# An attention-and-MLP kernel on one core: the halves of the weights are made by ScalarE and VectorE, GpSimd's casts go to other engines, and the planner that writes the order prices TensorE by the kind of product

## The chip, the cores and the metric

The kernel runs on one core of a Trainium2 chip. A core has five engines that run side by side, each with a queue of its own that is worked strictly in order: TensorE (PE in the profile, with its weight loads as PEld), VectorE (DVE), ScalarE (ACT), GpSimd (POOL) and SyncE (SP), which here only issues DMAs. The metric is the device time of one execution in microseconds (us), as the median of several runs.

## The reference

```python
def _attn_ref(q, k, v, M_prev, z_prev, beta):          # B, H, S, D = 4, 8, 576, 64
    scores = np.matmul(q, k.transpose(0, 1, 3, 2)) / np.sqrt(D)
    scores = np.where(np.triu(np.ones((S, S), bool), k=1), -1e9, scores)
    a = np.exp(scores - scores.max(-1, keepdims=True))
    a /= a.sum(-1, keepdims=True) + 1e-09
    local = np.matmul(a, v)
    q_p = np.where(q > 0, q, np.exp(q) - 1.0) + 1.0
    mem_out = (np.einsum('bhsd,bhde->bhse', q_p, M_prev)
               / (np.einsum('bhsd,bhd->bhs', q_p, z_prev)[..., None] + 1e-06))
    g = 1.0 / (1.0 + np.exp(-beta))[None, :, None, None]
    return g * mem_out + (1 - g) * local

def _moe_ref(x, w_in, w_out):                          # x: 2304 x 512, w_in: 512 x 2048, w_out: 2048 x 512
    h = x @ w_in
    return (h * np.cos(h)) @ w_out
```

The attention's output, laid out as 2304 tokens of 512 values, is the input x of the second part. Both weights come as 64-bit floats.

## The kernel before

**Stages and tiles.** The 2304 tokens are worked as nine chunks of 256: the first 64 rows of every head of all four batches (`small_pair`), then two chunks for each batch (`heads`, `scores`, `parts`, `local`, `memory`). While one job's attention is made, the second part (`moe_chunk`) runs for the chunks of the job before. A chunk is cut into eight **units** of 256 hidden columns, so that there are 72 units, counted from 1 here. Unit n is: a first product on TensorE into a PSUM bank `u` (`unit1`, L852); then a chain in `hidden`: ScalarE rounds (L873), VectorE subtracts (L875), ScalarE takes the sine (L877), VectorE multiplies by `u` (L879, the unit's **last multiply**), a cast makes the high half `gh` (by `copy`, L358 on ScalarE or L360 on the others) and a subtraction the low half `gl` (`sub`, L368); then a second product into `acc` (`unit2`, L894). There are two banks `u`, and a unit's last multiply still reads its bank: **the first product of unit n+2 cannot begin before the last multiply of unit n has ended.**

**Halves.** Eight chunks (64 units) use products of `fp32r` operands, each number cut in a high and a low half, three products for one. The first chunk (units 1 to 8, made while weights arrive) uses whole fp32 products. Each of 32 weight blocks is loaded as 64-bit words (`load_w`: DMA into `ws`; GpSimd's clamp L468; ScalarE L471; VectorE's shift L473; VectorE's join into `weight_val`, L478, from two SBUF tensors). `split_w` later cuts it into `weight_high` (L496 on ScalarE or L498 elsewhere) and `weight_low` (L503).

**Sine and exponential** need different tables on ScalarE, so a change between them costs an `ACT_TABLE_LOAD`.

**Order.** `Plan` collects all operations with the engines that may do each and a cost for each, and `order` lays them out by a simulated schedule; what comes out is the order in which every engine's queue is written, and which engine does each operation. `prm` has the numbers that steer it; `phi_on`, `gh_on` and `gl_on` are lists of the engines that may do a cast or a subtraction. A queue never reorders afterwards: a late operand holds all that stands behind it.

Of the kernel before, what the change touches and what calls it, by code (L numbers as in the profile page):

```python
# [37 lines left out]
class Op:  # L38
    __slots__ = ("on", "eng", "move", "tail", "share", "fn", "prio", "deps", "table", "idx", "start", "left", "outs", "at", "done", "cost", "port")
# [244 lines left out]
def kernel(  # L288
# [233 lines left out]
    def scores(prio, r, pair, qs, kcols, W, mk, nbs, sms, c):  # L522
# [5 lines left out]
        for k0 in range(0, W, n):  # L528
# [8 lines left out]
            P.op({"PE": 200 + 4 * mm(n)}, prod, prio, r=[pair], w=svs)  # L537
# [42 lines left out]
    def values(prio, stv, m, h, v2):  # L580
# [9 lines left out]
        def total(e):  # L590
            with nc.allow_low_precision("only the power of two next to the sum is used"):
# [4 lines left out]
             prio, r=[sums], w=[sv], after=[o_const], tail=106.0)  # L596
# [35 lines left out]
    def memory(prio, xbs, h0, nh, terms, reads, bank):  # L632
# [37 lines left out]
    def local(prio, rr, xbs, h, got, sm, r0, vals, mems):  # L670
# [140 lines left out]
    def emit_xT(prio, xbs, split):  # L811
# [7 lines left out]
        for b, xb in enumerate(xbs):  # L819
# [19 lines left out]
    def unit1(prio, i, bufs, views, split):  # L839

        u = P.buf("u")
        j, c0 = divmod(2 * i, 4)
        for f in range(2):
            cs = (c0 + f) * 128

            def prod(e, f=f, cs=cs):
# [39 lines left out]
    def unit2(prio, i, bufs, views, acc, split):  # L886
        for b in range(2):
# [211 lines left out]
```

## Time and profile before

| | |
|---|---|
| median of 3 runs | 611.62 us (608.96 to 611.73) |
| the profiled execution, own time | 612.86 us |
| its span, first to last instruction | 611.1 us |
| TensorE busy | 576.5 us, 94%, 4441 records |
| VectorE busy | 414.1 us, 68% |
| ScalarE busy | 367.9 us, 60% |
| GpSimd busy | 312.5 us, 51% |

Busy shares are averages over stages with different limits, so they name no bound by themselves. A VectorE or GpSimd row's duration includes time in which the instruction has been started and is held up.

### The profile page before, as it was taken

The numbers are of one execution on the slowest core, as the hardware profiler recorded it, in microseconds if no ns is written. First come the engines' busy times: TensorE is split into PE (matmuls) and PEld (weight loads), VectorE is DVE, ScalarE is ACT, GpSimd is POOL, SyncE is SP. The second block draws the span as 40 slices with busy tenths as digits, with TensorE's granted clock in tenths as the row PEclk, the third lists the DMA queues.
The fourth block names the chain that finished last, engine by engine and source line by source line (L and its number), as shares of the span: only waits on it lengthen the run. The fifth ranks groups of instructions, "written<-read, shape, count | busy, mean of one in ns | idle before, by whom it ended". The sixth has DMA issues, their size and how long they took to land.

```text
span 611.1 us, 12464 instructions
## 1 busy us (share of the span) xinstructions
PE 576.5 (94%) x4441; PEld 463.2 (76%) x4441; DVE 414.1 (68%) x1235; ACT 367.9 (60%) x798; POOL 312.5 (51%) x372
## 2 busy tenths in 40 slices
PE   6872699999999999999999999999999999999997
PEld 4661466567887877867987888888878889899996
DVE  3889989899788789887487856566878452322221
ACT  4857558688986788775576565576766532322321
POOL 3498477787665554653456263446453522332432
PEclk9876599999999999999999999999999999999999
DMA  8687885547663568548062843251833140000000
GB/s 277 212 207 217 252 243 157 106 86 172 142 136 69 145 143 150 118 98 178 19 149 64 158 84 84 39 136 49 146 58 85 39 64 1 35 1 1 35 1 35
DMA packets 121870, 67.07 MB, mean 110 GB/s; under 512 B 104656, under 2 KB 110288, under 8 KB 121808
## 3 DMA queue, kind: packets, MB, share of 16 engines
q1 hardware_dynamic: 121808, 66.28, 46.1%
q8 instruction: 35, 0.57, 0.4%
q14 instruction: 27, 0.22, 0.1%
HBM read 36.37 MB, written 4.72 MB: 67 GB/s over the span
## 4 chain that ended last, share of the span: by engine, by line
PE 83%; ACT 4%; DMA 4%; DVE 3%; issue 2%; POOL 2%; SPq 0%; POOLq 0%; ACTq 0%; DVEq 0%
PE u L852 33%; PE acc L894 32%; PE S L534 8%; PE pv L680 5%; PE mm L646 3%; DMA t<-p 2%; DMA ws<-in_w_in 2%; PE mm L824 1%; ACT s L549 1%; DVE p L562 1%; POOL wt L468 1%; DVE weight_val L478 1%; DVE wt L473 1%; SPq L371 0%; POOL weight_low L503 0%
## 5 line engine op out<-in xcount | busy, mean ns | idle before, releaser
L562 DVE SCALAR_TENSOR_TENSOR p<-s,p 128x64 f16<-128x64 f32 (+4 forms) x256 | 115.7, 489 | 18.9 <-POOL p L360 17.2
L852 PE MATMUL u<-xh,weight_high 128*128 128x256 f32 x416 | 120.5, 290 | 0.3 <-DVE w L879 0.3
L852 PE MATMUL u<-xl,weight_high 128*128 128x256 f32 x416 | 115.9, 279 | 0.0
L852 PE MATMUL u<-xh,weight_low 128*128 128x256 f32 x416 | 115.9, 279 | 0.0
L360 POOL TENSOR_SCALAR p<-s 128x320 f16<-128x320 f32 (+3 forms) x107 | 62.2, 586 | 97.0 <-ACT s L549 58.8
L360 POOL TENSOR_SCALAR gh<-w 128x512 fp32r<-128x512 f32 x58 | 38.2, 659 | 139.7 <-DVE w L879 94.9
L873 ACT ACTIVATE w<-u 128x512 int32<-128x512 f32 x72 | 42.7, 593 | 96.7 <-PE u L852 77.7
L894 PE MATMUL acc<-weight_high,gh 128*128 128x512 f32 x240 | 98.0, 409 | 0.0
L875 DVE SCALAR_TENSOR_TENSOR w<-w,u 128x512 f32<-128x512 int32 x72 | 48.9, 679 | 70.8 <-ACT w L873 70.8
L894 PE MATMUL acc<-weight_low,gh 128*128 128x512 f32 x240 | 94.5, 394 | 0.0
L894 PE MATMUL acc<-weight_high,gl 128*128 128x512 f32 x240 | 94.2, 393 | 0.0
L549 ACT ACTIVATE s<-s,nb 128x448 f32<-128x448 f32 (+3 forms) x128 | 77.8, 611 | 26.5 <-DVE nb L541 25.9
L852 PEld LDWEIGHTS u<-xh,weight_high 128*128 128x128 f32 x416 | 78.3, 188 | 10.7 <-issue 7.2
L368 POOL TENSOR_TENSOR gl<-w,gh 128x512 fp32r<-128x512 f32 x64 | 83.2, 1301 | 5.4 <-ACT gh L358 1.2
L852 PEld LDWEIGHTS u<-xl,weight_high 128*128 128x128 f32 x416 | 78.4, 188 | 1.0
L852 PEld LDWEIGHTS u<-xh,weight_low 128*128 128x128 f32 x416 | 78.5, 189 | 0.0
L534 PE MATMUL S<-stq 64*128 64x288 f32 (+3 forms) x320 | 66.3, 479 | 5.7 <-DVE nb L541 5.6
L541 DVE CUSTOM_DVE_ANT_0 s<-S,mask 128x320 f32<-128x320 f32 (+3 forms) x128 | 57.7, 474 | 18.6 <-PE S L534 18.1
L877 ACT ACTIVATE w<-w 128x512 f32<-128x512 f32 x72 | 45.1, 631 | 30.6 <-DVE w L875 30.3
L894 PEld LDWEIGHTS acc<-weight_high,gh 128*128 128x128 f32 x240 | 45.1, 188 | 16.4 <-issue 7.2
L879 DVE TENSOR_TENSOR w<-w,u 128x512 f32<-128x512 f32 x64 | 43.5, 680 | 19.9 <-ACT w L877 19.8
L680 PEld LDWEIGHTS <-t 128*128 128x128 f16 x1216 | 39.1, 98 | 18.1 <-issue 10.7
(116 smaller groups left out, 1093.4 us busy)
## 6 DMA issues: line engine op xcount, KB each, us to landing
ws<-in_w_in SPq DMA_DIRECT2D x16, 512.0 KB, 5.0
ws<-in_w_out SPq DMA_DIRECT2D x16, 512.0 KB, 3.9
stq<-in_qkp SPq DMA_DIRECT2D x12, 544.0 KB, 4.3
stv<-in_vk SPq DMA_DIRECT2D x16, 320.0 KB, 3.4
out<-w SPq DMA_DIRECT2D x16, 256.0 KB, 2.1
t<-p SPq DMA_TRANSPOSE x128, 3.2
mz<-in_mzp SPq DMA_DIRECT2D x20, 66.0 KB, 2.8
stq<-in_qkp SPq DMA_DIRECT2D x4, 288.0 KB, 3.4
```

Source lines behind the costliest of these rows:

```text
L360: eng[e].tensor_scalar(out=out, in0=in_, scalar1=scale, scalar2=1.0, op0=ALU.mult, op1=ALU.mult)
L368: lambda e: eng[e].tensor_tensor(out=out, in0=in0, in1=in1, op=ALU.subtract), prio, port=kw.pop('port', True), **kw)
L534: nc.tensor.matmul(out=sv.ap[:, 0:n], lhsT=pair.ap[p, qs], rhs=pair.ap[p, kcols + k0:kcols + k0 + n], start=True, stop=True)
L541: nc.vector.tensor_tensor_reduce(out=st.ap[:, k0:k0 + n], in0=sv.ap[:, 0:n], in1=mk[:, k0:k0 + n], scale=-1.0 / math.sqrt(D), scalar=above ...
L549: ex.append(P.op({"ACT": act(W, False, 2)}, lambda e, st=st, nb=nb, sm=sm: nc.scalar.activation(out=st.ap[:, 0:W], in_=st.ap[:, 0:W], func ...
L562: Pp({"DVE": dve(n)}, lambda e, c=c, n=n, to=to: nc.vector.scalar_tensor_tensor(out=pt.ap[:, to:to + n], in0=sa[:, c:c + n], scalar=PSCALE ...
L680: nc.tensor.matmul(out=pv.ap[:, 64 * i:64 * i + 64], lhsT=got[r].ap[:, block, :], rhs=vals.ap[:, part, h % 2, 64 * j:64 * j + 64], start=( ...
L852: nc.tensor.matmul(out=u.ap[:, f, :], lhsT=a[:, cs:cs + 128], rhs=x, start=(n == 0), stop=(n == len(terms) - 1))
L875: P.op({"DVE": dve(512)}, lambda e: nc.vector.scalar_tensor_tensor(out=wv, in0=wi, scalar=0.25, in1=u.ap, op0=ALU.subtract, op1=ALU.subtra ...
L877: P.op({"ACT": act(512, False)}, lambda e: nc.scalar.activation(out=wv, in_=wv, func=ACTF.Sin, scale=-TWO_PI_BELOW), ep, w=[w], table="sin")
L879: P.op({"DVE": dve(512)}, lambda e: nc.vector.tensor_tensor(out=wv if split else views[0], in0=wv, in1=u.ap, op=ALU.mult), ep, r=[u], w=[w ...
L894: nc.tensor.matmul(out=acc[b].ap, lhsT=a, rhs=w, start=(i == 0 and f == 0 and n == 0), stop=(2 * i + f == NF - 1 and n == len(terms) - 1))
```

## The change

It does four things. `some` and the new lists `hi_on`, `lo_on` and `clamp_on` fix who cuts the weights: ScalarE makes every high half, VectorE every low half, GpSimd keeps the clamps. The casts of `parts` and `hidden` (`phi_on`, `gh_on`) may no longer go to GpSimd. In the planner, a change of TensorE between kinds of product (`SWITCH`, whole fp32, halves, scores, small fp16) now has a price whenever the kind changes, and several costs are set anew. And the steering numbers in `prm` are others. The computation is the same.

```diff
+SWITCH = {"h": 0.0, "v": 15.0}
...
-                back = e == "PE" and tail == 80.0 and o.tail != 80.0
+                back = e == "PE" and o.kind != kind
...
             if e == "PE":
-                if o.tail != 80.0:
-                    cost += tail
-                tail = o.tail
+                cost += SWITCH.get(o.kind, 95.0) if o.kind != kind else 0.0
+                kind = o.kind
...
+    def some(on, name):
+        return {e: on[e] for e in on if e in prm[name]}
...
-        P.op({"Pool": pool(512), "DVE": dve(512)}, lambda e: eng[e].tensor_scalar(
+        Pp(some({"Pool": pool(512), "DVE": dve(512)}, "clamp_on"), lambda e: eng[e].tensor_scalar(
...
-        o = P.op({"ACT": act(512, False), "DVE": dve(512, True), "Pool": pool(512)}, high, prio,
-                 after=[w_ready[key], *left_by.get(ph, list)()])
-        w_ready[key] = Pp({"DVE": dve(512), "Pool": 1240}, low, prio, after=[o, *left_by.get(pl, list)()])
+        o = Pp(some({"ACT": act(512, False), "DVE": dve(512, True), "Pool": pool(512)}, "hi_on"), high, prio,
+               after=[w_ready[key], *left_by.get(ph, list)()])
+        w_ready[key] = Pp(some({"DVE": dve(512), "Pool": 1240}, "lo_on"), low, prio, after=[o, *left_by.get(pl, list)()])
...
-    "xt": 12.861,
...
+    "xt": 24.853,
...
-    "phi_on": ('ACT', 'Pool', 'DVE'),
-    "gh_on": ('ACT', 'Pool', 'DVE'),
+    "phi_on": ('ACT', 'DVE'),
+    "gh_on": ('ACT', 'DVE'),
     "gl_on": ('DVE', 'Pool'),
+    "hi_on": ('ACT',),
+    "lo_on": ('DVE',),
+    "clamp_on": ('Pool',),
```

The built programs show who does what now. GpSimd's queue falls from 372 rows to 176: its casts by `copy` from 175 to 19, its high and low halves of weights (12 and 32) to none. ScalarE's casts by `copy` rise from 41 to 176 and its high halves from 20 to 32; its table loads fall from 56 to 50 and its scalings of `x` (L666) from 96 to 60. VectorE gets 32 low halves, 21 casts, 18 scalings of two heads at once (L662) and 5 instructions of L623. TensorE has the same 4057 products in both, in 293 runs of one kind before and 297 now. DMAs are the same in number. Lines of the changed kernel are 3 to 9 higher than those of before (L885 is L879 of before, L883 is L877, L509 is L503, L474 is L468).

GpSimd's queue from its fourth clamp on, before (`wt` is the block being made from `ws`, `p` an attention tile, `stv` and `v` a tile of values):

```order
L468 TENSOR_SCALAR wt_139<-ws_137 128x512
L498 TENSOR_SCALAR weight_high<-weight_val 128x512
L503 TENSOR_TENSOR weight_low<-weight_val,weight_high 128x512
L498 TENSOR_SCALAR weight_high<-weight_val 128x512
L360 TENSOR_SCALAR p_90<-s_78 128x320
L468 TENSOR_SCALAR wt_138<-ws_134 128x512
L503 TENSOR_TENSOR weight_low<-weight_val,weight_high 128x512
L360 TENSOR_SCALAR p_92<-s_74 128x192
L468 TENSOR_SCALAR wt_139<-ws_135 128x512
```

and the same place of the change:

```order
L474 TENSOR_SCALAR wt_139<-ws_137 128x512
L474 TENSOR_SCALAR wt_138<-ws_134 128x512
L474 TENSOR_SCALAR wt_139<-ws_135 128x512
L474 TENSOR_SCALAR wt_138<-ws_136 128x512
L474 TENSOR_SCALAR wt_139<-ws_137 128x512
L474 TENSOR_SCALAR wt_138<-ws_134 128x512
L474 TENSOR_SCALAR wt_139<-ws_135 128x512
L610 TENSOR_SCALAR stv_67<-stv_67,vs_108 128x384
L363 TENSOR_SCALAR v_72<-stv_67 128x2x192
```

The halves and casts that stood between the clamps have left the queue, so a clamp follows the clamp before.

ScalarE's queue around the first sine, before (`w_102` and `w_103` are the tiles of units 1 and 2; the rounding of unit 1, L873, stands 30 rows ahead of its sine, and 18 of the 32 weight blocks' L471 stand ahead of it):

```order
L358 ACTIVATE p_92<-s_74 128x192
L549 ACTIVATE s_75,sm_121<-s_75,nb_117 128x192
L592 ACTIVATE v_72,va_113<-stv_67 128x385
L877 ACT_TABLE_LOAD
L877 ACTIVATE w_102<-w_102 128x512
L471 ACTIVATE wt_138<-wt_138 128x512
L877 ACTIVATE w_103<-w_103 128x512
```

and in the change, where 12 of the L471 (now L477) stand ahead of it:

```order
L361 ACTIVATE p_93<-s_75 128x192
L879 ACTIVATE w_102<-u_128 128x512
L627 ACTIVATE e_69<-stq_66 128x256
L477 ACTIVATE wt_139<-wt_139 128x512
L632 ACTIVATE e_69<-e_69 128x256
L883 ACT_TABLE_LOAD
L883 ACTIVATE w_102<-w_102 128x512
L477 ACTIVATE wt_138<-wt_138 128x512
L502 CAST weight_high<-weight_val 128x512
```

The sine of unit 1 has moved up to five rows behind its rounding.

VectorE's queue around the last multiply of unit 8 (the sixth row), before (`xl` is the low half of the next chunk's input, the ISA rows are the maxima of scores):

```order
L879 TENSOR_TENSOR t_88<-w_102,u_128 128x512
L541 ISA s_87,nb_114<-S_130,mask,nb_114 128x288
L541 ISA nb_114 128x1
L473 TENSOR_SCALAR wt_139<-wt_139 128x512
L368 TENSOR_TENSOR xl_101<-mm_133,xh_100 128x4x128
L879 TENSOR_TENSOR t_89<-w_103,u_129 128x512
L478 SCALAR_TENSOR_TENSOR weight_val<-ws_137,wt_139 128x512
L541 ISA s_86,nb_115<-S_131,mask,nb_115 128x288
```

and from that multiply on in the change:

```order
L885 TENSOR_TENSOR t_89<-w_103,u_129 128x512
L509 TENSOR_TENSOR weight_low<-weight_val,weight_high 128x512 x2
L371 TENSOR_TENSOR xl_101<-mm_133,xh_100 128x4x128
L547 ISA s_87,nb_114<-S_130,mask,nb_114 128x288
L547 ISA nb_114 128x1
L547 ISA s_86,nb_115<-S_131,mask,nb_115 128x288
L547 ISA nb_115 128x1
L509 TENSOR_TENSOR weight_low<-weight_val,weight_high 128x512 x2
```

Low halves stand there now, where none was. Ahead of the last multiply of unit 13, VectorE's two lists differ by 26 low halves, 6 scalings of two heads (12 for 6) and one cast more, and by one each of L875, L628, L601 and L575 less. Ahead of the first product of unit 15 TensorE's lists differ by 25 small products of `local` (204 for 229), and ahead of that of unit 19 by nothing but their order.

## Rows read from the trace of the kernel before

**Rows 1.** The page, part 1: busy time, share of the span and instructions of each engine.

```profile
PE 576.5 (94%) x4441; PEld 463.2 (76%) x4441; DVE 414.1 (68%) x1235; ACT 367.9 (60%) x798; POOL 312.5 (51%) x372
```

**Rows 2.** Busy time of each engine in four stretches; the columns are the stretch, its length, busy us (and instructions) of TensorE, its weight loads, VectorE, ScalarE and GpSimd, the granted clock, the share of the DMA engines' time, and GB/s.

```profile
37.00:69.30 32.30, 15.05 (x72) 10.80 (x72) 28.63 (x55) 20.86 (x45) 26.51 (x27) 0.66 0.77 218
69.30:169.30 100.00, 98.34 (x609) 68.72 (x610) 88.89 (x237) 74.43 (x157) 68.92 (x74) 0.97 0.65 160
169.30:287.60 118.30, 116.69 (x1033) 90.77 (x1032) 99.54 (x338) 87.63 (x194) 62.92 (x77) 1.00 0.60 129
287.60:500.00 212.40, 212.40 (x1806) 177.41 (x1804) 143.53 (x459) 132.29 (x280) 102.08 (x124) 1.00 0.43 86
```

**Rows 3.** TensorE in order of time, around the first product of unit 3: start, length, line, tiles, count and, in brackets, the idle time ahead and what ended it.

```profile
63.39 0.58 PE L680 MATMUL pv<-v,t 128*128 128x64 f16 x8 [3.35 <-DVE x L687]
...
69.30 6.59 PE L852 MATMUL u<-s,weight_val 128*128 128x256 f32 x16 [3.05 <-DVE t L879]
```

**Rows 4.** ScalarE in order of time, 42 to 70 us: the rounding of unit 1, the twelfth L471, and the first sine with its table load.

```profile
42.67 0.60 ACT L873 ACTIVATE w<-u 128x512 int32<-128x512 f32 x1 [0.80 <-PE u L852]
...
50.14 0.63 ACT L471 ACTIVATE wt<-wt 128x512 f32<-128x512 f32 x1 [0.22 <-POOL wt L468]
...
66.60 1.28 ACT L877 ACT_TABLE_LOAD   x1
67.89 0.63 ACT L877 ACTIVATE w<-w 128x512 f32<-128x512 f32 x1
```

**Rows 5.** VectorE in order of time, 43 to 71 us: a shift and a join held up, the last multiply of unit 1, and a shift, a division and a join that are not held up.

```profile
45.31 1.49 DVE L473 TENSOR_SCALAR wt<-wt 128x512 int32<-128x512 int32 x1
...
47.51 1.76 DVE L478 SCALAR_TENSOR_TENSOR weight_val<-ws,wt 128x512 int32<-128x512 int32 x1
...
68.56 0.69 DVE L879 TENSOR_TENSOR t<-w,u 128x512 f32<-128x512 f32 x1 [1.03 <-ACT w L877]
...
69.29 0.42 DVE L473 TENSOR_SCALAR wt<-wt 128x512 int32<-128x512 int32 x1
69.63 0.22 DVE L562 SCALAR_TENSOR_TENSOR p<-s,p 128x64 f16<-128x64 f32 x1
69.76 0.68 DVE L478 SCALAR_TENSOR_TENSOR weight_val<-ws,wt 128x512 int32<-128x512 int32 x1
```

**Rows 6.** VectorE, the last multiply of unit 13, and TensorE, the first product of unit 15, each in order of time.

```profile
168.62 0.68 DVE L879 TENSOR_TENSOR w<-w,u 128x512 f32<-128x512 f32 x1
174.70 0.28 PE L852 MATMUL u<-xh,weight_high 128*128 128x256 f32 x1
```

**Rows 7.** Busy time in three more stretches, columns as in rows 2.

```profile
30.00:169.30 139.30, 116.96 (x700) 81.92 (x700) 124.52 (x301) 100.31 (x214) 101.72 (x108) 0.89 0.68 175
134.90:151.00 16.10, 14.70 (x135) 11.47 (x133) 14.73 (x43) 14.32 (x32) 11.99 (x12) 1.00 0.76 162
0.00:287.60 287.60, 256.74 (x1921) 189.24 (x1922) 241.76 (x730) 208.00 (x473) 176.06 (x212) 0.93 0.66 164
```

**Rows 8.** Groups by form, VectorE from 0 to 150.9 us and GpSimd from 0 to 169.3 us; count | busy us, mean ns of one | idle before, and what ended it.

```profile
L478 DVE SCALAR_TENSOR_TENSOR weight_val<-ws,wt 128x512 int32<-128x512 int32 x32 | 32.4, 1014 | 0.0
L473 DVE TENSOR_SCALAR wt<-wt 128x512 int32<-128x512 int32 x32 | 19.2, 600 | 2.2 <-ACT wt L471 2.2
L562 DVE SCALAR_TENSOR_TENSOR p<-s,p 128x64 f16<-128x64 f32 x23 | 11.3, 493 | 0.7 <-ACT p L358 0.7
L875 DVE SCALAR_TENSOR_TENSOR w<-w,u 128x512 f32<-128x512 int32 x11 | 7.4, 676 | 1.6 <-ACT w L873 1.6
L575 DVE TENSOR_SCALAR sm<-sm,vs 128x2 f32<-128x2 f32 x10 | 5.7, 578 | 0.0
L503 POOL TENSOR_TENSOR weight_low<-weight_val,weight_high 128x512 fp32r<-128x512 f32 x28 | 38.9, 1391 | 2.6 <-PE acc L894 1.4 <-DMA t<-p 0.5 <-ACT weight_high L496 0.5
L468 POOL TENSOR_SCALAR wt<-ws 128x512 f32<-128x512 f32 x32 | 24.2, 757 | 28.7 <-DMA ws<-in_w_in 11.1 <-DVE weight_val L478 9.5 <-DMA ws<-in_w_out 5.2
L498 POOL TENSOR_SCALAR weight_high<-weight_val 128x512 fp32r<-128x512 f32 x10 | 7.0, 700 | 4.6 <-DMA ws<-in_w_in 1.6 <-DVE weight_val L478 1.6 <-PE mm L595 0.7
L360 POOL TENSOR_SCALAR p<-s 128x320 f16<-128x320 f32 x5 | 2.9, 588 | 1.9 <-ACT s L549 1.8
```

**Rows 9.** Groups by form over the whole span, of operations that the change adds or takes away; columns as in rows 8.

```profile
L368 DVE TENSOR_TENSOR xl<-mm,xh 128x512 fp32r<-128x512 f32 x16 | 11.0, 689 | 13.8 <-ACT xh L835 13.8
L662 DVE TENSOR_TENSOR x<-mm,r 128x128 f32<-128x128 f32 x20 | 4.8, 282 | 0.1
L680 PE MATMUL pv<-v,t 128*128 128x64 f16 x1216 | 43.4, 194 | 9.2 <-DMA t<-p 5.9 <-DVE x L687 3.3
L358 ACT ACTIVATE p<-s 128x320 f16<-128x320 f32 x7 | 3.2, 462 | 3.2 <-DMA t<-p 3.2
L496 ACT CAST weight_high<-weight_val 128x512 fp32r<-128x512 f32 x18 | 11.0, 612 | 4.7 <-DVE weight_val L478 4.2 <-POOL wide_both L503 0.5
L666 ACT ACTIVATE x<-mm,r 128x64 f32<-128x64 f32 x88 | 20.1, 310 | 2.5 <-DVE r L656 1.8 <-PE pv L680 0.5
L877 ACT ACT_TABLE_LOAD x28 | 35.9, 1283 | 0.5
```

**Rows 10.** ScalarE in order of time, the sine of unit 25, and TensorE, the first product of unit 27.

```profile
286.62 0.63 ACT L877 ACTIVATE w<-w 128x512 f32<-128x512 f32 x1
289.27 0.37 PE L852 MATMUL u<-xh,weight_high 128*128 128x256 f32 x1
```

More of the change, by code (lines that the diff above doesn't have):

```diff
@@ L38 @@
 class Op:
-    __slots__ = ("on", "eng", "move", "tail", "share", "fn", "prio", "deps", "table", "idx", "start", "left", "outs", "at", "done", "cost", "port")
+    __slots__ = ("on", "eng", "move", "kind", "share", "fn", "prio", "deps", "table", "idx", "start", "left", "outs", "at", "done", "cost", "port")
 ENGINES = ("PE", "DVE", "ACT", "Pool", "SP")
@@ L96, in buf, with op @@
         return made[-1]
-    def op(self, on, fn, prio, r=(), w=(), a=(), after=(), move=None, table=None, tail=0.0, share=1.0, port=False):
+    def op(self, on, fn, prio, r=(), w=(), a=(), after=(), move=None, table=None, kind="f", share=1.0, port=False):
         o = Op()
-        o.on, o.move, o.fn, o.prio, o.table, o.tail, o.share, o.port = on, move, fn, prio, table, tail, share, port
+        o.on, o.move, o.fn, o.prio, o.table, o.kind, o.share, o.port = on, move, fn, prio, table, kind, share, port
         deps = set(after)
@@ L194, in forward @@
         skipped = dict.fromkeys(engines, 0.0)
-        clock, queues, tail = Clock(), 0.0, 0.0
+        clock, queues, kind = Clock(), 0.0, None
         port = 0.0
@@ L535, in prod @@
                                      rhs=pair.ap[p, kcols + k0:kcols + k0 + n], start=True, stop=True)
-            P.op({"PE": 200 + 4 * mm(n)}, prod, prio, r=[pair], w=svs)
+            P.op({"PE": 194 + 4 * mm(n)}, prod, prio, kind="s", r=[pair], w=svs)
             for i, (sv, st, nb) in enumerate(zip(svs, sts, nbs)):
@@ L595, in values @@
         P.op({"PE": 3}, lambda e: nc.tensor.matmul(out=sv.ap[:, 0:1], lhsT=ones.to_broadcast([128, 128]), rhs=sums.ap, start=True, stop=True),
-             prio, r=[sums], w=[sv], after=[o_const], tail=106.0)
+             prio, r=[sums], w=[sv], after=[o_const], kind="v")
         o = P.op({"DVE": 100}, lambda e: nc.vector.tensor_scalar(
@@ L646, in prod @@
                     nc.tensor.matmul(out=mb.ap[p, c], lhsT=a, rhs=b, start=True, stop=True)
-        P.op({"PE": 10 + 4 * n / 2.4 * nb if whole else 610 + fm * mm(256)}, prod, prio, r=reads, w=[mb],
+        P.op({"PE": 1.38 * n * nb if whole else 610 + fm * mm(256)}, prod, prio, r=reads, w=[mb],
              share=1.0 if whole else (240 + fm * mm(256)) / (610 + fm * mm(256)))
@@ L682, in prod @@
                                      stop=(n == len(terms) - 1))
-        P.op({"PE": 3 + 29 * sum(3 * r + 2 for r in rr)}, prod, prio, r=[vals, *(got[r] for r in rr)], w=[pv], tail=80.0)
+        P.op({"PE": 3 + 29 * sum(3 * r + 2 for r in rr)}, prod, prio, r=[vals, *(got[r] for r in rr)], w=[pv], kind="h")
         for i, r in enumerate(rr):
@@ L824, in tr @@
                     nc.tensor.transpose(mb.ap[:, k * 128:(k + 1) * 128], xb.ap[:, k * 128:(k + 1) * 128], ident)
-            P.op({"PE": 440}, tr, prio, r=[xb], w=[mb], after=[o_const])
+            P.op({"PE": 358}, tr, prio, r=[xb], w=[mb], after=[o_const])
             mv = mb.ap.rearrange("p (k t) -> p k t", k=KD)
@@ L853, in prod @@
                                      stop=(n == len(terms) - 1))
-            o = P.op({"PE": 1380 if split else 1728}, prod, prio, r=bufs, w=[u],
+            o = P.op({"PE": 1368 if split else 1718}, prod, prio, kind="r" if split else "f", r=bufs, w=[u],
                      after=[w_ready["i", j, k] for k in range(KD)])
@@ L1009 @@
 prm = {
-    "v": -0.17,
-    "step": 1.238,
-    "pv": 2,
-    "xt": 12.861,
-    "ew": 0,
-    "u2": 13.132,
+    "v": -0.833,
+    "step": 1.165,
+    "pv": 1.318,
+    "xt": 24.853,
+    "ew": 0.517,
+    "u2": 13.369,
     "w0": -4.023,
-    "wdt": 18.984,
-    "small": 3.264,
-    "t0": 80,
+    "wdt": 23.471,
+    "small": 4.859,
+    "t0": 55.948,
     "dtu": 5.006,
     "dth": 2.0,
-    "lead": 0.917,
-    "mem": 3.906,
+    "lead": 0,
+    "mem": 4.581,
     "switch": 1300.0,
-    "patience": 60,
-    "hold": 24.207,
-    "bdve": 1140.609,
+    "patience": 19.426,
+    "hold": 32.243,
+    "bdve": 1238.886,
     "bact": 440.469,
     "ws": 0,
-    "s0": -60,
-    "rounds": 6,
+    "s0": -69.122,
+    "rounds": 11,
     "nwt": 2,
-    "glue": 0,
-    "portw": 3.0,
+    "glue": -0.185,
+    "portw": 13.204,
     "group": 4,
     "clamps": 'p',
-    "lazy": 4000,
+    "lazy": 4288.524,
     "wide": 23,
```

4 lines of the change are left out of this document (2 added, 2 removed).

## The prediction

> **What bounds the kernel now.** I read the busy times first. TensorE is busy 576.5 us of the 611.1 us span [rows 1], so the time is TensorE's work plus the waits inside it. The stretches then say where the waits are [rows 2]: from 37 to 69.3 us TensorE works 15.1 of 32.3 us, at a granted clock of 0.66 (a mixture of its two levels, 1.2 and 2.4 GHz), from 69.3 to 169.3 us it works 98.3 of 100, and from 287.6 to 500 us all 212.4. From 75 us on it is a queue that nearly always has work; whatever moves the end must move that queue as a whole.
>
> What starts the full stretch is seen in order of time. Unit 3's first product starts at 69.30 us, after 3.05 us idle, released by a last multiply [rows 3]. This is unit 1's. Its sine ran at 67.89, behind a table load at 66.60, though its rounding was done at 43.3 [rows 4], and the multiply at 68.56 [rows 5]: for 23 us it stood in ScalarE's list behind other work, weight blocks (L471) among it. The twelfth L471 ran at 50.14 [rows 4]; 18 stand ahead of the sine.
>
> TensorE being full after 75 us doesn't mean that VectorE has time to spare. A unit's first product waits for a last multiply two units back, and when the list is laid out tightly the slack is small. Unit 13's last multiply ended at 169.30 and unit 15's first product, which waits for it, started at 174.70 [rows 6]: 5.4 us. So VectorE is nearly as full as TensorE there: from 30 to 169.3 us it is busy 124.5 of 139.3 us, idle 10.6%; in its tightest part, 134.9 to 151 us, 14.73 of 16.10, idle 8.5% [rows 7].
>
> Part of that busy time is being held up. A join (L478) takes 1.76 us and a shift (L473) 1.49 where GpSimd works, and 0.68 and 0.42 at 69 us, when nothing is in the way [rows 5]. To 150.9 us the means are 1014 ns for 32 joins and 600 for 32 shifts, 493 for 23 small divisions (L562; 220 free [rows 5]), 578 for 10 tiny ones (L575; I take 220 as for L562) [rows 8]: 32 x 0.334 + 32 x 0.18 + 23 x 0.273 + 10 x 0.358 = 10.7 + 5.8 + 6.3 + 3.6 = 26.4 us.
>
> **The change part by part.** *The early start.* In the new list the sine of unit 1 stands 5 rows behind its rounding and behind 12 L471. If the rounding ends near 43.3 and the twelfth L471 near 50.8 as now [rows 4], the multiply is done near 49 to 51 and unit 3 may start some 18 to 20 us before 69.3. By itself that is a lead of up to 20 us; only what cannot hold the lead takes it away again.
>
> *VectorE has to keep up with it.* Up to the last multiply of unit 13 its list gains 26 low halves; the nearest row of that shape is the low half `xl`, 689 ns [rows 9]: 17.9 us. Six more scalings of two heads at 0.282 [rows 9] are 1.7; one cast is bounded by nothing and the 0.69 us of the same shape, I take 0.3. One each of four small kinds fewer (0.68 for L875 [rows 8], the others bounded by 0.22 and 0.6) take 2.1 off. Sum +17.8 us.
>
> *What GpSimd no longer does.* To 169.3 us it loses 32 low halves at 1391 ns (44.5), 12 high halves at 700 (8.4) [rows 8] and about ten casts at 0.6 (6): 59 us. Its clamps stay, 32 at 757 ns. How much of VectorE's held-up time goes with them I bound from two sides. Held-up time of 26.4 us against 101.7 us of GpSimd's work [rows 7] is 0.26 us for each; 59 us less gives 15. If instead a low half holds up an instruction of VectorE by 1.07 us, as at 45 and 47 us (1.49 less 0.42, 1.76 less 0.68 [rows 5]), 26 of them give 28. I take the middle, 22, since the four groups aren't all that is held up but low halves don't always meet something.
>
> *The sum.* VectorE from 30 us to the multiply of unit 13: 124.5 + 17.8 - 22 = 120.3 us of work. With 10% idle, as now, that lasts 133.7 us and ends at 163.7 instead of 169.3. The multiply no longer has 5.4 us of slack, since TensorE with 20 us lead is waiting: unit 15 starts at 163.8, 10.9 us earlier than 174.70. TensorE's list ahead of it is 25 small products of `local` shorter (25 x 43.4/1216 = 0.9 [rows 9]), which come later: a lead of 10.0 us that is worth anything. So TensorE gets 20 us of lead near 50 us and loses half of it, in waits for last multiplies between about 110 and 165 us.
>
> Behind unit 15, six low halves remain for VectorE, which is 4 us, and its shares fall (99.5 of 118.3 us, then 143.5 of 212.4 [rows 2]). TensorE's work after it is the same set of products. I count its 297 runs of one kind against 293 as nothing: from 287.6 to 500 us it turns from kind to kind and is still busy all the time [rows 2]. The DMAs are the same in number and their share falls from 0.77 to 0.43 [rows 2].
>
> *ScalarE.* To the sine of unit 25 (286.62 us [rows 10]) it gains some 58 casts, at 0.46 (320 wide) to 0.61 us (512 wide) [rows 9]: 32; 12 high halves at 0.612: 7.3; it loses 24 scalings at 0.31, 7.4, and six table loads at 1.283, 7.7. Together +24 on 208.0 us of 287.6 [rows 7]. The cover is the idle time of 79.6 us. With the lead of 10 us, it would have to do 232 in 277 us, idle 45; I count it at nothing, and take it up as a rival.
>
> *Sum of it all.* Span 611.1 - 10.0 = 601.1 us. The profiled execution's own time is 612.86, 1.8 over its span and 1.2 over the median of 611.62: so own 602.9 and a median near **601.5 us**. With relief of 15 and 10% idle, VectorE's work is 127.3 us, the multiply ends at 171.4 and the gain is 174.7 - 171.5 - 0.9 = 2.3 (609). With 28 and 8% idle it is 114.3, ends at 154.2, gain 19.5 (592).
>
> **The rivals.** *A: VectorE keeps up.* Low halves go into the idle 10%, or the relief is the full 28: the whole 20 us stays, span 591, median about 591.5. For it: a lead of 20 us moves VectorE's work earlier too, where it has some slack (28.6 of 32.3 us busy from 37 to 69.3 [rows 2]; little). Against it: the 8.5% of the tightest part [rows 7], which looks like a floor.
>
> *B: the low halves wait as the joins do.* A join reads two SBUF tensors and takes 1014 ns on average; L875 of the same shape has one operand in PSUM and takes 676 over the same stretch [rows 8]. `xl`, my row for the low half, also reads PSUM; the low half on VectorE reads `weight_val` and `weight_high`, both in SBUF. At 1014 instead of 689, 26 cost 8.5 us more, which makes 128.8 us of work, ends at 173.1, and gives unit 15 at 173.3: 1.4 less 0.9, so 0.5 us, and a median of 611. Against it: what the joins wait for is mostly the low halves that GpSimd no longer makes; only clamps are left to collide with. The Trainium skill, "SBUF — State Buffer", section "Who interferes with whom", says that VectorE and GpSimd share one pair of SBUF ports under an exclusive lock; by that rule two engines working on SBUF tensors take turns and a half moved to VectorE would not be free of waits while clamps run. The rows of joins at 1.76 beside and 0.68 us free agree with it, and by it alone the sum would lie between mine and this rival's.
>
> *C: slower, ScalarE.* The casts of `gh` may go to ScalarE or VectorE alone, and GpSimd no longer catches what is late. The place is the stretch up to unit 25's sine; unit 27's first product starts at 289.27, 2.0 us after that sine's end [rows 10]. With 232 us of work it is late as soon as its idle time there is above 57 us of the present 79.6 (289 - 232). ScalarE now idles 28% (79.6 of 287.6); at 22.5% it would end at 232 / 0.775 = 299, ten late: span 621, median 621. For it: a queue in strict order idles when an operand is late, and each `gh` cast waits for a multiply of a VectorE that I hold to be the bound. Against: its idle time is mostly not on the chain now, since from 169.3 us on TensorE is kept full while ScalarE idles a quarter (87.6 of 118.3 busy [rows 2]).
>
> *D: the early start does not come.* The first 12 L471 wait for clamps, and these for `ws` from DMA; if blocks land late, unit 3 stays near 60 to 65 us. That costs nothing as long as it takes less than the half of the lead that I count as lost anyway; it belongs to the lower half of my own range.
>
> **How the numbers follow.** My forecast (VectorE paces units 11 to 24, gain 2 to 19 us) 0.57, A 0.15, B 0.16, C 0.12. Within 0.5%, about what a measurement of this kernel can tell from no change, is 608.6 to 614.7. Faster is A and my own case but for 0.02 at its upper end: 0.70. Slower is C but for 0.02 of mild delays, and 0.02 of B, where some of C meets it: 0.12. The rest is the same: 0.18. The range has to leave out no more than 2 in 10: from 590, under A, to 612, over B; C is left out, as is a tail below.
>
> **What would show it.** The early start: unit 3's first product near 50 us, and the full clock well before 75 us. The relief: joins at 750 to 800 ns instead of 1014, shifts near 450 instead of 600, GpSimd busy 160 to 190 us instead of 312.5. The price: low halves near 0.69 us each (1.0 is B). The pacing: TensorE's longest waits between 110 and 165 us, released by a last multiply (L885), and unit 15 at about 164. If unit 15 starts there at 155, it is A. After it TensorE should need the same 436 us to the end (611.1 - 174.7); if it needs more, with waits behind sines or `gh` casts between 170 and 290 us, C is right. My forecast would be wrong most easily in the relief, which is a difference of two bounds far apart, and in taking TensorE's work as unchanged when its order is not.

## The result and the profile after

The changed kernel takes 588.58 us (median of 4 runs, 587.38 to 590.20) against 611.67 (608.96 to 613.57): a ratio of 0.9627, 95% interval 0.9584 to 0.9671. That is 23 us faster, where 10 were forecast with a range of 590 to 612. The profiled execution took 588.59 us, with a span of 586.9.

The page, part 1 and the clock row of part 2, answering to [rows 1]:

```profile
PE 568.5 (97%) x4441; PEld 457.7 (78%) x4441; DVE 402.8 (69%) x1311; ACT 415.6 (71%) x898; POOL 171.5 (29%) x172
...
PEclk9989999999999999999999999999999999999999
```

Windows of the changed kernel, columns as in [rows 2], the same four stretches, and four up to the last multiply of unit 13, which now ends at 146.6 us, to set beside [rows 7]:

```profile
37.00:69.30 32.30, 29.32 (x151) 20.65 (x150) 28.19 (x72) 24.19 (x51) 13.83 (x17) 1.00 0.94 270
69.30:169.30 100.00, 99.06 (x743) 70.87 (x742) 94.57 (x287) 88.90 (x186) 35.32 (x34) 1.00 0.61 145
169.30:287.60 118.30, 116.12 (x1034) 93.01 (x1033) 97.13 (x352) 97.49 (x220) 35.61 (x30) 1.00 0.64 130
287.60:500.00 212.40, 210.08 (x1759) 176.35 (x1758) 133.38 (x443) 144.57 (x302) 55.76 (x46) 1.00 0.38 76
0.00:30.00 30.00, 23.83 (x207) 16.82 (x208) 22.64 (x113) 24.14 (x81) 7.99 (x25) 0.97 0.88 289
30.00:146.60 116.60, 112.67 (x704) 79.29 (x702) 106.24 (x312) 98.56 (x208) 43.81 (x49) 0.98 0.77 198
0.00:146.60 146.60, 136.51 (x909) 96.11 (x909) 128.88 (x424) 122.70 (x287) 51.81 (x74) 0.98 0.79 216
110.00:146.60 36.60, 36.60 (x315) 29.23 (x311) 34.81 (x107) 33.30 (x65) 13.50 (x11) 1.00 0.62 137
```

The kernel before had up to the same multiply, and in its first 30 us:

```profile
0.00:30.00 30.00, 23.09 (x191) 16.55 (x191) 17.70 (x95) 20.06 (x69) 11.42 (x28) 0.89 0.75 249
0.00:169.30 169.30, 140.05 (x890) 98.47 (x891) 142.22 (x395) 120.37 (x281) 113.14 (x135) 0.89 0.69 188
```

From 37 to 69.3 us TensorE works 29.3 us instead of 15.1, at a granted clock of 1.00 instead of 0.66, so at 2.4 GHz throughout. Most of the time came from this stretch. From 110 us to the multiply TensorE is busy all the time, and VectorE 34.81 of 36.60 us; the next wait of TensorE for a last multiply comes behind 169.3 us (0.8 us, once). From 169.3 to 500 us TensorE is busy a little less than before, so something was given back there.

ScalarE in order of time, from the rounding of unit 1 over the twelfth L477 to the sine (before: [rows 4]):

```profile
39.87 0.58 ACT L879 ACTIVATE w<-u 128x512 int32<-128x512 f32 x1
...
40.66 0.62 ACT L477 ACTIVATE wt<-wt 128x512 f32<-128x512 f32 x1
...
41.60 1.28 ACT L883 ACT_TABLE_LOAD   x1
42.89 0.63 ACT L883 ACTIVATE w<-w 128x512 f32<-128x512 f32 x1
```

TensorE in order of time, the first products of units 1, 3 and 4 (the second answers to [rows 3]):

```profile
31.61 5.44 PE L858 MATMUL u<-s,weight_val 128*128 128x256 f32 x16
...
44.91 3.62 PE L858 MATMUL u<-s,weight_val 128*128 128x256 f32 x16
...
51.79 1.46 PE L858 MATMUL u<-s,weight_val 128*128 128x256 f32 x6
```

The sine starts 3 us after its rounding instead of 25, and the twelfth L477 runs at 40.66 us instead of 50.14 [rows 4]. Unit 1 starts 5.3 us earlier (31.61 against 36.92), unit 3 24.4 us earlier, and its product takes 3.62 us instead of 6.59, so unit 4 starts 27.4 us earlier (51.8 against 79.2).

VectorE by form, 0 to 150.9 us (before: [rows 8]):

```profile
L484 DVE SCALAR_TENSOR_TENSOR weight_val<-ws,wt 128x512 int32<-128x512 int32 x32 | 22.5, 704 | 0.0
L509 DVE TENSOR_TENSOR weight_low<-weight_val,weight_high 128x512 fp32r<-128x512 f32 x23 | 17.5, 780 | 0.0
L479 DVE TENSOR_SCALAR wt<-wt 128x512 int32<-128x512 int32 x32 | 14.5, 456 | 7.2 <-ACT wt L477 7.0
L881 DVE SCALAR_TENSOR_TENSOR w<-w,u 128x512 f32<-128x512 int32 x14 | 9.5, 678 | 0.3 <-ACT w L879 0.2
L568 DVE SCALAR_TENSOR_TENSOR p<-s,p 128x64 f16<-128x64 f32 x29 | 7.2, 248 | 2.0 <-ACT p L361 1.9
```

Joins fell from 1014 to 704 ns, nearly the 0.68 us of a free one, shifts from 600 to 456, and small divisions from 493 to 248. L881, which reads one operand from PSUM, is where it was (678 against 676). The low halves take 780 ns in the mean.

VectorE, a low half and the last multiply of unit 13, and TensorE, the first product of unit 15, in order of time (before: [rows 6]):

```profile
145.35 0.69 DVE L509 TENSOR_TENSOR weight_low<-weight_val,weight_high 128x512 fp32r<-128x512 f32 x1
145.96 0.68 DVE L885 TENSOR_TENSOR w<-w,u 128x512 f32<-128x512 f32 x1
```
```profile
145.98 1.02 PE L540 MATMUL S<-stq 64*128 64x448 f32 x4
146.94 0.39 PE L858 MATMUL u<-xh,weight_high 128*128 128x256 f32 x1
```

Unit 15 starts 27.8 us earlier, 0.3 us behind the multiply, and without a wait: TensorE is at work on scores until then. From there to the end of the span it takes 440.0 us instead of 436.4.

### The profile page after: what moved, and what is told of

It is laid out like the page before. It is cut to its first block, busy times and chain, and to the rows that moved or that the text cites. A ratio compares the mean times of both kernels' runs of the same rounds, so it can differ in the third digit from the quotient of the medians.

```text
span 586.9 us, 12402 instructions
## 1 busy us (share of the span) xinstructions
PE 568.5 (97%) x4441; PEld 457.7 (78%) x4441; DVE 402.8 (69%) x1311; ACT 415.6 (71%) x898; POOL 171.5 (29%) x172
## 4 chain that ended last, share of the span: by engine, by line
PE 66%; ACT 13%; DMA 9%; DVE 6%; issue 3%; POOL 1%; ACTq 0%; POOLq 0%; SPq 0%; DVEq 0%
PE u L858 27%; PE acc L900 26%; DMA t<-p 6%; PE S L540 5%; PE pv L686 4%; ACT s L555 3%; ACT p L361 2%; DVE p L568 2%; PE mm L652 2%; DMA ws<-in_w_out 1%; DVE s L547 1%; ACT wt L477 1%; DMA stv<-in_vk 1%; ACT L883 1%; DMA ws<-in_w_in 1%
## 5 line engine op out<-in xcount | busy, mean ns | idle before, releaser
L568 DVE SCALAR_TENSOR_TENSOR p<-s,p 128x64 f16<-128x64 f32 (+4 forms) x256 | 93.0, 403 | 11.1 <-ACT p L361 10.1
L881 DVE SCALAR_TENSOR_TENSOR w<-w,u 128x512 f32<-128x512 int32 x72 | 49.2, 683 | 73.3 <-ACT w L879 73.3
L555 ACT ACTIVATE s<-s,nb 128x192 f32<-128x192 f32 (+3 forms) x128 | 77.8, 609 | 5.3 <-DVE nb L547 5.0
L879 ACT ACTIVATE w<-u 128x512 int32<-128x512 f32 x72 | 42.5, 590 | 52.2 <-PE u L858 44.5
L361 ACT ACTIVATE p<-s 128x320 f16<-128x320 f32 (+3 forms) x114 | 55.2, 504 | 15.7 <-DMA t<-p 15.6
L540 PE MATMUL S<-stq 64*128 64x288 f32 (+3 forms) x320 | 64.8, 473 | 0.6 <-DVE nb L547 0.6
L885 DVE TENSOR_TENSOR w<-w,u 128x512 f32<-128x512 f32 x64 | 43.7, 684 | 25.6 <-ACT w L883 25.1
L883 ACT ACTIVATE w<-w 128x512 f32<-128x512 f32 x72 | 45.2, 631 | 21.8 <-DVE w L881 21.5
L361 ACT ACTIVATE gh<-w 128x512 fp32r<-128x512 f32 x57 | 35.7, 628 | 26.7 <-DVE w L885 18.9
L900 PEld LDWEIGHTS acc<-weight_low,gh 128*128 128x128 f32 x240 | 45.1, 188 | 9.7
```

The source lines that it names most:

```text
L361: nc.scalar.activation(out=out, in_=in_, func=ACTF.Copy, scale=scale)
L540: nc.tensor.matmul(out=sv.ap[:, 0:n], lhsT=pair.ap[p, qs], rhs=pair.ap[p, kcols + k0:kcols + k0 + n], start=True, stop=True)
L555: ex.append(P.op({"ACT": act(W, False, 2)}, lambda e, st=st, nb=nb, sm=sm: nc.scalar.activation(out=st.ap[:, 0:W], in_=st.ap[:, 0:W], func ...
L568: Pp({"DVE": dve(n)}, lambda e, c=c, n=n, to=to: nc.vector.scalar_tensor_tensor(out=pt.ap[:, to:to + n], in0=sa[:, c:c + n], scalar=PSCALE ...
L879: P.op({"ACT": act(512)}, lambda e: nc.scalar.activation(out=wi, in_=u.ap, func=ACTF.Copy, bias=0.25), ep, r=[u], w=[w])
L881: P.op({"DVE": dve(512)}, lambda e: nc.vector.scalar_tensor_tensor(out=wv, in0=wi, scalar=0.25, in1=u.ap, op0=ALU.subtract, op1=ALU.subtra ...
```

## The experiments

Two questions were put: does the early start last by itself, or only because VectorE got time back; and how much work could VectorE and ScalarE still take. Six kernels change the lists, the numbers or the pricing and let the planner lay the order out anew; the six others keep an order and change only who issues an instruction, or how often. Their ratios are to the kernel before in the same series (612 us).

The form of the edits in an unchanged order (here for the low halves; `high` and `"ACT"` answer to it elsewhere):

```diff
     with tc.manual_schedule():
+        for o in seq:
+            if o.fn.__name__ == "low":
+                o.eng = "Pool"
         for o in seq if not DRY else []:
             o.fn(o.eng)
```

**New lists alone, laid out anew** (`hi_on`, `lo_on`, `clamp_on`, `phi_on`, `gh_on` of the change, with `some` that reads them, put into the kernel before):

```diff
...
-    "phi_on": ('ACT', 'Pool', 'DVE'),
-    "gh_on": ('ACT', 'Pool', 'DVE'),
+    "phi_on": ('ACT', 'DVE'),
+    "gh_on": ('ACT', 'DVE'),
+    "hi_on": ('ACT',),
+    "lo_on": ('DVE',),
+    "clamp_on": ('Pool',),
```

> The kernel before with the new lists of engines alone (ScalarE makes the high halves, VectorE the low ones, GpSimd only clamps, no casts on GpSimd); steering numbers and the pricing of TensorE's changes of kind are those of before, and the planner lays the list out anew. Theory 1 (relief: what GpSimd no longer does frees VectorE, and that lets an early start last): most of the gain comes, 587 to 595 us, joins near 0.7 us, unit 3 starting at 45 to 52 us. Theory 2 (the steering numbers make the early start, VectorE had room anyhow): 603 to 612 us.

596.87 us, ratio 0.9754 (0.9732 to 0.9776): 15.3 us faster, between the two expectations and nearer to the first. Laid out anew with the old numbers, the new lists bring the sine of unit 1 to 47.2 us and unit 3 to 48.6, so the early start does not need the new numbers, and joins take 737 ns.

**New numbers and pricing alone, laid out anew** (the change with the lists of before):

```diff
-    "phi_on": ('ACT', 'DVE'),
-    "gh_on": ('ACT', 'DVE'),
+    "phi_on": ('ACT', 'Pool', 'DVE'),
+    "gh_on": ('ACT', 'Pool', 'DVE'),
...
-    "hi_on": ('ACT',),
-    "lo_on": ('DVE',),
-    "clamp_on": ('Pool',),
+    "hi_on": ('ACT', 'Pool', 'DVE'),
+    "lo_on": ('DVE', 'Pool'),
+    "clamp_on": ('Pool', 'DVE'),
```

> The changed kernel (its steering numbers and its pricing of changes of kind) with the old lists of engines: GpSimd may make halves and casts again. In its list the sine of unit 1 stands 4 rows behind the rounding. Theory 1: the early start comes but does not last, VectorE is held up by some 40 us to unit 13 as before; 599 to 608 us, joins near 1.0 us. Theory 2: 587 to 592 us.

605.54 us, ratio 0.9899 (0.9863 to 0.9935). ScalarE from the rounding to the sine of unit 1, and VectorE by form to 150.9 us:

```profile
38.72 0.60 ACT L879 ACTIVATE w<-u 128x512 int32<-128x512 f32 x1 [1.11 <-PE u L858]
40.36 1.28 ACT L883 ACT_TABLE_LOAD   x1
41.65 0.63 ACT L883 ACTIVATE w<-w 128x512 f32<-128x512 f32 x1
```
```profile
L484 DVE SCALAR_TENSOR_TENSOR weight_val<-ws,wt 128x512 int32<-128x512 int32 x32 | 28.2, 886 | 0.0
L479 DVE TENSOR_SCALAR wt<-wt 128x512 int32<-128x512 int32 x32 | 19.7, 618 | 6.5 <-ACT wt L477 6.4
L568 DVE SCALAR_TENSOR_TENSOR p<-s,p 128x64 f16<-128x64 f32 x24 | 9.6, 398 | 0.2 <-POOL p L363 0.2
```

The sine is as early as in the change, and unit 4 starts 25.0 us earlier than before. But joins and divisions are held up, and at unit 9 (122.7 us against 129.3) only 6.6 us of that is left.

**The engines of the halves alone, order of before** (low halves issued by VectorE, high halves by ScalarE):

```diff
+        for o in seq:
+            if o.fn.__name__ == "low":
+                o.eng = "DVE"
+            if o.fn.__name__ == "high":
+                o.eng = "ACT"
         for o in seq if not DRY else []:
             o.fn(o.eng)
```

> The kernel before with its order as it is, only the low halves are issued by VectorE and the high halves by ScalarE at the same places. Both theories: the late start of unit 3 is in the list (its sine behind 18 weight blocks), so it stays between 58 and 70 us, and from there TensorE is full; the gain is no more than what TensorE waits after it, about 6 us: 604 to 611 us. If it is under 600, the late start itself came from held-up time, not from the order.

614.88 us, ratio 1.0048 (1.0032 to 1.0064), 2.7 us slower, where 1 to 8 us faster were expected. VectorE by form to 150.9 us, its last multiply of unit 13, and TensorE's first product of unit 3:

```profile
L478 DVE SCALAR_TENSOR_TENSOR weight_val<-ws,wt 128x512 int32<-128x512 int32 x32 | 22.3, 698 | 0.0
...
L562 DVE SCALAR_TENSOR_TENSOR p<-s,p 128x64 f16<-128x64 f32 x23 | 6.5, 285 | 0.6 <-ACT p L358 0.6
```
```profile
169.47 0.68 DVE L879 TENSOR_TENSOR w<-w,u 128x512 f32<-128x512 f32 x1
```
```profile
67.30 5.72 PE L852 MATMUL u<-s,weight_val 128*128 128x256 f32 x16 [3.13 <-DVE t L879]
```

Here the relief is nearly whole (698 and 285 ns), and it buys nothing: unit 3 still waits for its late sine, and unit 13's multiply ends at 170.1 us against 169.3, although VectorE is busy only 79.9 of the 95.1 us from 75 us to it: TensorE, busy 90.2 of them, doesn't bring its unit any earlier. So with the order of before, VectorE is not the bound. The casts stayed on GpSimd in this run; all engines of the change in the order of before were not tried.

**Low halves on GpSimd, order of the change:**

> The changed kernel with its order as it is, only the 32 low halves are issued by GpSimd instead of VectorE at the same places. Theory 1: VectorE loses 26 x 0.69 = 18 us of work up to unit 13's multiply and gets about 29 us of held-up time back, so it is some 11 us late there: 597 to 602 us. Theory 2: no more than 2 us of difference, 587 to 591 us.

596.02 us, ratio 0.9733 (0.9715 to 0.9751), 7.4 us above the change. **High halves on GpSimd, order of the change:**

> The changed kernel with its order as it is, only the 32 high halves are issued by GpSimd instead of ScalarE (0.70 us each, one SBUF tensor read). Theory 1a (any work of GpSimd on SBUF holds VectorE up by its own length): 22 us of GpSimd's work hold VectorE up by 10 us or more, 593 to 600 us, joins near 0.8 us. Theory 1b (what holds it up are the low halves, which read two tensors and take 1.39 us): 587 to 592 us, joins below 0.75 us.

591.96 us, ratio 0.9655 (0.9621 to 0.9690), by time not to be told from the change. **Low halves and casts on GpSimd, order of the change:**

> The changed kernel with its order as it is; GpSimd makes the low halves and all of ScalarE's casts of p and of values (GpSimd has 134 casts, 175 before). VectorE is then held up nearly as before, some 30 to 40 us to unit 13, with the early start kept. Theory 1: 600 to 607 us. If the time ScalarE gets back counts more: 590 to 597 us.

607.97 us, ratio 0.9938 (0.9910 to 0.9966). The windows of these three up to the end of unit 13's multiply, in this order, columns as in [rows 2]:

```profile
0.00:153.50 153.50, 137.76 (x908) 97.43 (x909) 128.45 (x398) 123.22 (x289) 85.64 (x100) 0.98 0.77 206
```
```profile
0.00:151.80 151.80, 139.81 (x909) 98.26 (x909) 134.45 (x424) 110.58 (x262) 75.35 (x102) 0.96 0.79 208
```
```profile
0.00:158.00 158.00, 140.03 (x908) 98.29 (x909) 133.75 (x398) 114.00 (x262) 101.63 (x127) 0.96 0.73 200
```

Beside 128.88 us of VectorE and 51.81 of GpSimd in the change: with the low halves gone VectorE has 26 x 0.69 = 17.9 us less to do and is yet busy 128.45, so it is held up 17.5 us more, 0.67 for each of the 26. With the high halves on GpSimd it is held up 134.45 - 128.88 = 5.6 us more; the casts add 133.75 - 128.45 = 5.3. The three make 28.4 us. A low half costs VectorE the same whether it makes it or GpSimd does; the 7 us that the first of these runs lost are idle time (25.1 us up to that multiply against 17.7), and so latency, not work.

**Every low half made twice by VectorE** (the instruction is issued a second time):

```diff
-            eng[e].tensor_tensor(out=wl[key], in0=wv[key], in1=wh[key].bitcast(F32), op=ALU.subtract)
+            for _ in range(2):
+                eng[e].tensor_tensor(out=wl[key], in0=wv[key], in1=wh[key].bitcast(F32), op=ALU.subtract)
```

> The changed kernel, every low half of a weight made twice by VectorE (26 of the 32 ahead of unit 13's last multiply, 0.69 us each: 18 us of work more there). Theory 1 (VectorE sets the pace of units 11 to 24 once the early start is there; unit 15 now starts 0.3 us behind the multiply that it waits for): idle time covers a part, 8 to 16 us slower, 597 to 605 us. Rival (VectorE's idle 17.6 us up to that multiply is room): within 3 us, 587 to 592 us.

610.65 us, ratio to the kernel before 0.9969 (0.9947 to 0.9992), 22.1 us above the change (20.9 by the two ratios, give or take 3) for 32 x 0.69 = 22.1 us of work: slower than either expectation. VectorE and TensorE in order of time at unit 13's multiply and unit 15's first product, and the window from 110 us to that multiply, columns as in [rows 2]:

```profile
163.36 1.41 DVE L510 TENSOR_TENSOR weight_low<-weight_val,weight_high 128x512 fp32r<-128x512 f32 x2
164.69 0.68 DVE L886 TENSOR_TENSOR w<-w,u 128x512 f32<-128x512 f32 x1
```
```profile
163.06 1.45 PE L541 MATMUL S<-stq 64*128 64x448 f32 x4 [1.48 <-DVE nb L548]
165.43 0.38 PE L859 MATMUL u<-xh,weight_high 128*128 128x256 f32 x1 [0.91 <-DVE w L886]
```
```profile
110.00:165.40 55.40, 45.39 (x344) 35.44 (x343) 54.81 (x137) 40.62 (x80) 16.59 (x13) 0.97 0.49 105
```

Within the noise all added work arrives at the end. Up to this multiply VectorE is busy 21.4 us more and 18.7 us later; little goes into its idle time (15.1 us, 17.7 in the change). From 110 us on it now paces TensorE, busy 54.81 of 55.40 us while TensorE works 45.39. In the change TensorE waits for nothing there: VectorE has next to nothing to spare, but it is not what TensorE waits for.

**Every high half made twice by ScalarE:**

```diff
                 nc.scalar.copy(out=wh[key], in_=wv[key])
+                nc.scalar.copy(out=wh[key], in_=wv[key])
```

> The changed kernel, every high half of a weight made twice by ScalarE (32 x 0.6 = 19 us of work more, nearly all ahead of unit 20). Theory 1 (VectorE paces, ScalarE has room): 0 to 4 us slower, 588 to 593 us. Rival (ScalarE, which gained 48 us of work, is the bound of the first half): 10 to 19 us slower, 598 to 608 us.

599.94 us, ratio 0.9805 (0.9776 to 0.9834): 11.4 us above the change, give or take 3, for 32 x 0.6 = 19 us of work. This lies between the two expectations, nearer to the rival's. TensorE's waits from 45 to 200 us, and VectorE's from 30 us to the multiply of unit 13 (us in total, times, longest):

```profile
PE u L859 <- DVE w L886: 4.1, 4, 1.5
PE pv L687 <- DMA t<-p: 2.5, 2, 1.9
PE mm L602 <- DVE x L669: 2.2, 2, 2.0
```
```profile
DVE wt L479 <- ACT wt L477: 7.5, 4, 4.6
DVE w L882 <- ACT w L880: 3.1, 4, 2.0
DVE t L886 <- ACT w L884: 2.3, 1, 2.3
```

TensorE waits longest for last multiplies (0.8 us in the change), and VectorE waits for ScalarE's rounding (3.1 us, 0.2 in the change) and sine (2.3) ahead of them: ScalarE too has little room.

**The pricing of before in the change, laid out anew** (a price behind small fp16 and summing products only, in the ranking as in the cost):

```diff
-                back = e == "PE" and o.kind != kind
+                back = e == "PE" and kind == "h" and o.kind != "h"
...
-                cost += SWITCH.get(o.kind, 95.0) if o.kind != kind else 0.0
+                cost += {"h": 80.0, "v": 106.0}.get(kind, 0.0) if o.kind != "h" else 0.0
```

> The changed kernel, only the pricing of TensorE's changes of kind is that of before (a price behind small fp16 and summing products alone). TensorE's work is 538 us in both; theory 1 needs only the early sine (13 rows into the same place) and the new engines: 586 to 594 us. Rival (the pricing gives a part of the gain by fewer or better placed changes): 595 to 602 us.

591.28 us, ratio 0.9657 (0.9637 to 0.9676): as the first theory expected, and not clear of the change. Unit 1 starts at 35.2 us instead of 31.6 and unit 15 at 155.1 instead of 146.9, yet no more than 2.7 us are lost at the end: in another layout, the start of one unit is no measure of the time.

**Casts back on their old lists; halves and clamps back on theirs; low halves on GpSimd alone,** each laid out anew from the change:

> The changed kernel, its casts of p and gh may go to GpSimd again as before; the halves stay with ScalarE and VectorE; laid out anew. Theory H (the halves' move makes nearly all of the relief): 588 to 594 us. Theory K (the casts' move makes it): 598 to 604 us.

600.60 us, ratio 0.9836 (0.9765 to 0.9907), as theory K expected, with runs from 597 to 606 us.

> The reverse: the changed kernel, the halves and clamps may be made by the engines of before (28 low and 11 high halves go to GpSimd), the casts stay off GpSimd; laid out anew. Theory H: 597 to 604 us, as with the new numbers alone. Theory K: 588 to 594 us. With low halves costing VectorE as much by being in GpSimd's way (0.67 us each in the run with the low halves on GpSimd) as by being made there (0.69): 594 to 598 us.

617.16 us, ratio 1.0085 (1.0058 to 1.0112), slower than the kernel before and outside all three expectations.

> The changed kernel, the low halves made by GpSimd alone and the order laid out for that. If the 7 us lost with the low halves on GpSimd in an unchanged order come from a place in the order that doesn't suit GpSimd's 1.39 us: 588 to 592 us. If they come from the engines: 594 to 598 us.

610.51 us, ratio 0.9971 (0.9948 to 0.9995), outside both expectations. These three answer less than they were meant to. The last was laid out for GpSimd's low halves and is 14 us slower than the same move in an unchanged order: it starts unit 3 at 52.7 us instead of 45.2 and waits 7.0 us once for a multiply. A new layout moves the time by as much as the engines do, so halves against casts is not settled by them. In the unchanged order both count: the low halves on GpSimd cost 7.4 us, the casts another 12. The change was laid out anew as well, so how much of its 23 us is a layout that came out well is not shown.

Set side by side, from the order of time of each run (us; "busy" is VectorE's up to the end of unit 13's multiply):

| | unit 1 | unit 3 | unit 9 | unit 13's multiply ends | VectorE busy | unit 15 | median |
|---|---|---|---|---|---|---|---|
| before | 36.9 | 69.3 | 129.3 | 169.3 | 142.2 | 174.7 | 611.67 |
| after | 31.6 | 44.9 | 106.2 | 146.6 | 128.9 | 146.9 | 588.58 |
| lists alone, anew | 34.6 | 48.6 | 112.7 | 159.8 | 139.3 | 159.9 | 596.87 |
| numbers alone, anew | 32.0 | 50.7 | 122.7 | 162.7 | 137.5 | 164.8 | 605.54 |
| engines alone, order of before | 37.0 | 67.3 | 130.0 | 170.1 | 137.9 | 175.5 | 614.88 |
| low halves twice | 32.2 | 45.7 | 110.5 | 165.4 | 150.3 | 165.4 | 610.65 |

## Why the prediction was wrong

**The early start and the relief came, both larger than forecast; the step that failed is the one by which VectorE takes half the lead back.** The prediction had TensorE wait for last multiplies between about 110 and 165 us and lose 10 of 20 us there. In the change it waits for nothing in that stretch, and its lead is 24.4 us at unit 3 and 27.8 at unit 15. Of the signs that the prediction named, the joins (704 ns) and GpSimd's 171.5 us came, the waits did not, and unit 15 came ahead even of the 155 us that it gave to rival A. Behind the step stands the sum that put unit 13's multiply at 163.7 us; it ended at 146.6, 17.1 us earlier. By its terms, the largest miss being the relief:

- *Added work, 17.8 us:* right within what can be read; a free low half takes 0.69 us, 780 ns in the mean.
- *Relief, 22 us between 15 and 28:* it was 142.2 + 17.8 - 128.9 = 31.1 us, above my upper bound. This is 9.1 of the 17.1. The lower bound spread the held-up time of four groups evenly over GpSimd's work. The upper one looked at low halves alone, at 1.07 us, and counted 26, those that VectorE gains; but all 32 had been on GpSimd ahead of that multiply (28 in [rows 8] and four into `wide_both`), which makes 34. The runs show 0.67 us for a low half, and some 0.2 us for a high half (5.6 us for 28) or a cast (5.3 for 27). For the 32 low halves, 12 high halves and 17 casts (ten in the prediction) that left GpSimd there, this makes 21.4 + 2.4 + 3.4 = 27 of the 31 us; the rest is not placed.
- *Up to 30 us as before:* VectorE had done 22.64 us by then instead of 17.70 (the rows of before above), 4.9 us that the prediction did not look for, since it took the first chunk's order as unchanged. With the old pricing 3.6 of the 5.3 us by which unit 1 starts earlier are gone, as far as one new layout can tell.
- *Idle 10%:* it was 10.4 of 116.6, 8.9%, which gives 3.0 us against 13.4 forecast.

Together 9.1 + 4.9 + 3.0 = 17.0. (The prediction's last step, 602.9 - 1.2, is 601.7 and not 601.5; nothing hangs on it.)

**The early start, 18 to 20 us,** was 24.4 at unit 3 and 27.4 at unit 4. The prediction left the twelfth weight block at about 50 us "as now". It ran at 40.66, 9.5 us earlier, and the rounding 2.8 us earlier. This is the order's doing and not GpSimd's relief: with the low halves back on GpSimd in the new order the block runs at 40.2 us, with the halves moved in the old order at 49.3. The 3 us between units 3 and 4 are the clock, which I named as a sign and didn't price: in [rows 3] unit 3's product ran 6.59 us after long idle stretches of TensorE, and now 3.62.

**Rival A** (VectorE keeps up, the whole lead stays, 591) is what came, and by the condition it named, a relief of at least 28. Its "against", the 8.5% of idle as a floor, did not hold: VectorE idles 4.9% from 110 to 146.6 us (34.81 of 36.60 busy) and 1.1% in the run with doubled low halves (54.81 of 55.40). Most of the miss is still relief and early work, 14.0 of 17.0 us; 3.0 are idle time.

**Rival B** (low halves wait as joins do) fell: 780 ns, not 1014, so 23 x 0.09 = 2 us instead of 8.5. The page that stood beside it, "SBUF — State Buffer" in the Trainium skill, section "Who interferes with whom", describes taking turns on one port pair. The runs agree in direction: low halves beside the clamps take 780 ns for a free 690, and the trade of a low half is even for VectorE, 0.69 against 0.67 us.

**Rival C** (ScalarE) did not decide, but some 0.6 of every microsecond added to ScalarE is lost, so my "counted at nothing" was too easy. Of the 27.8 us that unit 15 is early, 3.6 are given back later, 0.9 of them the 25 moved products. The waits behind the rest (`xh` of ScalarE 1.0 us, `x` of VectorE 0.8, scores 0.6, a last multiply 0.8) are small and of several kinds; no single cause was shown.

**That VectorE was nearly as full as TensorE before** is the reading I would take back. Unit 13's multiply came 5.4 us ahead of unit 15 with VectorE 10% idle; the run with relief in the old order shows it coming at about the same time with VectorE idle 32.2 us up to it instead of 27.1. Only with TensorE 27 us early does VectorE run close to full.

## What to carry to other kernels

A late start and a held-up engine can hide each other: the halves' relief in the old order bought nothing, and the early start without relief was mostly lost again by the ninth unit. Where the planner could use the relief, the new lists alone gained 15.3 us; with the 6.6 of the new numbers this is nearly the 23 of both. So when an edit makes two moves, cost each with the other already done. To learn whether an engine has room, issue a known instruction twice in an unchanged order: 22 us of work that returned as 21 to 22 us settled what idle shares could not. That it has no room does not yet make it the bound; for that, look at what TensorE waits for in the kernel itself. When a planner lays the order out, change engines without letting it plan again, or the layout's own scatter (14 us here) covers the effect.

## What the runs showed that was not expected

GpSimd's work holds VectorE up by different amounts: 17.5 us for 33.8 us more of low halves (two SBUF tensors read), 5.6 for 23.5 of high halves and 5.3 for 16.0 of casts (one tensor read), so 0.52, 0.24 and 0.33 us for each microsecond; VectorE's L881 (L875 before), with one operand in PSUM, takes 679 to 683 ns over the whole span in every run.
